# A separate account for row maxima beside a two-layer MLP, and a later division: a gated mix of sliding-window attention and MLP

## The chip, the cores and the metric

The kernel runs on one core of one Trainium2 chip. The metric is the device time of one execution in microseconds (us), lower is better. TensorE (PE, with its weight loads PEld), VectorE (DVE), ScalarE (ACT) and GpSimd (POOL) compute; SyncE (SP) issues the DMAs in the order of the program.

## The reference

The input is a sequence of 2048 rows of 512 values in fp32. Two branches are computed and mixed row by row with a gate.

```python
g = sigmoid((x * gate_w).sum(-1, keepdims=True))
# A: attention, 32 heads of 16, each query sees itself and the 255 keys before it
q, k, v = heads(x @ wqkv)                       # wqkv 512 x 1536
p = softmax(where(mask, q @ k.T * 16 ** -0.5, -1e9))
a = merge(p @ v) @ wo                           # wo 512 x 512
# B: MLP, hidden width 1792
h = gelu_tanh(x @ w1 + b1)
b = h @ w2 + b2
return g * a + (1 - g) * b
```

## The kernel before

**Staging.** The rows are cut in four tiles of 512. Large products run as three matmuls on a high and a low half of each operand (`mm3`, L108 to L110): first q, k and v of all tiles (`qkv`), then the MLP in eight turns of half the hidden width and one tile each (`mlp`), then the product with `wo` (`final`). A turn has two stages. In the first, u, seven blocks of x times w1 are made, and each goes through `gelu` (L715): four steps on ACT and three on DVE (L725, L731, L737). In the second, y, the seven results are multiplied with w2 into four output blocks, which DVE evicts (L812). `stage[0]` tells which of the two is being issued.

**Attention.** It is issued between these products, in 128 blocks: eight head groups of four heads, each over 16 blocks of 128 rows. A block has four steps, and for each step there are two things. `att_max` (L508) makes a score product `sm` (L519) on PE whose row maximum DVE takes (L524, into `M`); `att_exp` (L553) makes a score product `st` (L564) with the maximum already subtracted, whose exponential ACT takes (L586, into `pt`), and POOL masks it (L580; in the last blocks DVE does, L574). When four blocks of maxima are complete, `att_rows` (L530) turns them into rows of the second operand `qs`: three steps on DVE (L536 to L539), then eight copies on POOL (L546). `att_pvs` (L592) multiplies the exponentials of six blocks with v once in four blocks, into two accumulators, `pv_st` and `pv_sm`, which ACT and DVE evict into `nd` (L629, L632). `sm` and `st` have three PSUM buffers each, and a `pv` accumulator takes one of each kind.

**Division.** After two head groups `att_norm` (L642) divides: load the denominators (`den`, L646), reciprocal on DVE (L650, step `rcp`), store (L653, `keep`), load numerators and reciprocals (L658, `back`), multiply on DVE (L662, `mul`), store (L665). When each comes after the load of `den` stands in `DIVS` in nanoseconds, in one row for the last of the four passes and in one for the others. `load_part` (L695) loads the finished product `ot` (L703) and casts it into two halves on ACT (L706) and DVE (L709); for tile 0 the casts are planned `LAND0` after the load.

**Order.** The order on each engine is written out when the program is built. A planner keeps a clock, `now`, that each matmul advances by its planned length (`tick`); `after(ns, fn)` puts a step into a heap, and it is issued on its engine as soon as the clock passes its due time. The main loop goes through the steps of the blocks, and after each lets the dense products go on for a quarter of `STEP` (`fill`). In y and in the q, k, v stage it goes by pairs: both steps' scores, then both shares of dense work; in u each step stands alone. The block of maxima is always `LEAD` = 12 blocks ahead of the block of exponentials, so exactly one `sm` goes with one `st`. For the first 12 blocks there are maxima alone. The loads of `kd` and `qd`, the operands of `sm`, are issued by the block of maxima, those of `ks` and `vbuf` by the block of exponentials.

Of the kernel before, what the change touches and what calls it, by code (L numbers as in the profile page):

```python
# [19 lines left out]
NT = S // T  # L20
NB = T // 128
# [11 lines left out]
def gated_mix(ctx: ExitStack, tc: tile.TileContext, x, wqkv, wo, w1, b1, w2, b2, gate_w, out):  # L33
# [448 lines left out]
    def load_kd(g_, c):  # L482
        for t in range(max(c - 1, 0), c + 1):
            ready(t, g_, 1)
            k0 = 0 if t == c else T - W
            at = W if t == c else 0
            src = heads(SK[t], g_)[:, :, :, :, k0:].rearrange("s d u a c -> (s d u) a c")
            nc.sync.dma_start(f32(kd[0:96, slot(g_, c), :, at:at + T - k0]), src)

    def load_qd(g_, c):  # L490
        ready(c, g_, 0)
        put_pairs([f32(qd[48 * s:48 * s + 48, slot(g_, c)]) for s in range(2)], SQ[c], g_)

    def load_qs(g_, c):
        ready(c, g_, 0)
        need(("v", NT - 2, NB - 1))
        for s in range(2):
            v = f32(qs[64 * s + 4:64 * s + 52, :, c * T:(c + 1) * T])
            nc.sync.dma_start(v, part(SQ[c], g_, s).rearrange("r (a c) -> r a c", a=2))
# [8 lines left out]
    def att_max(g_, b, i):  # L508

        if b % RB == 0 and (g_, b // RB) not in Ms:  # L510
            Ms[g_, b // RB] = sb.tile([128, 2 * RB, 2], F32, tag="M", bufs=2, name=f"M{g_}_{b}")
        M = Ms[g_, b // RB]
        hb, pr = divmod(i, 2)
        c, n = b // NB, slot(g_, b // NB)
        j = 2 * (b % NB) + hb
        w = min(64 * (2 * b + hb + 1), W + 64)
        k1 = 64 * (j + 1) + W
        p = ps.tile([128, 320], F32, tag="sm", bufs=3, name=f"sm{g_}_{b}_{i}")
        nc.tensor.matmul(p[:, :w], qd[0:96, n, pr, 128 * j:128 * (j + 1)], kd[0:96, n, pr, k1 - w:k1],  # L519
                         start=True, stop=True)  # L520
        junk = cs.tile([128, 320], BF16, tag="jm", bufs=1, name=f"jm{g_}_{b}_{i}")

        def red():
            nc.vector.tensor_tensor_reduce(junk[:, :w], p[:, :w], mask[:, 320 - w:320], 1.0, -3e38,  # L524
                                           ALU.add, ALU.max, M[:, 2 * (b % RB) + hb, pr:pr + 1])
            done.add(("max", g_, b, i))
        tick(w / 2.4 + 13)
        after(100, red)
# [376 lines left out]
    stage = ["qk"]  # L905
# [3 lines left out]
    def fill(ns):  # L909

        owed[0] += ns
        while owed[0] > 0:
            c = next(run)
            if c is None:
                owed[0] = -1e9
            else:
                owed[0] -= c
                tick(c)

    NU = NG * NKB  # L920
    NQ = NG * NT
    fill(START - AHEAD)
    for c in (0, 1):
        load_qd(0, c)
    fill(AHEAD)
    for u in range(-LEAD, NU):
        m = u + LEAD
        gm, bm = divmod(m, NKB)
        step = STEP if u >= 0 else STEP0
        for i in range(4):  # L930
            if i == 1 and m % NB == 0 and NB <= m < NU - NB:
                load_kd(*divmod(m // NB + 1, NT)), load_qd(*divmod(m // NB + 1, NT))
            if i % 2 == 0:
                pair = (i, i + 1) if stage[0] != "u" else (i,)
            elif len(pair) == 2:
                continue
            else:
                pair = (i,)
            for op, i in [(op, k) for k in pair for op in ORDER[:3]] + [("f", k) for k in pair]:
                if op == "s" and u >= 0:  # L940
                    att_exp(u // NKB, u % NKB, i)
                if op == "m" and m < NU:
                    att_max(gm, bm, i ^ XOR)
                if op == "p" and i == PVAT and u >= 1:
                    att_pvs(u - 1)
                if op == "f":
                    fill(step / 4)
        if m < NU and bm % RB == RB - 1:
            after(900, att_rows, gm, bm // RB)
        if m % NB == QAT % NB and QAT <= m < QAT + NKB:  # L950
            load_qs(0, (m - QAT) // NB)
        if u % NB == 0 and NB <= u < NU - NB:
            load_ks(*divmod(u // NB + 1, NT))
        if u % NB == 2 and NB < u < NU - 3 * NB:
            load_qs(*divmod(u // NB + 3, NT))
        if u % NB == 0 and u >= 0:
# [14 lines left out]
RB = 4  # L971
NKB = S // 128
# [3 lines left out]
LEAD = 12  # L976
QAT = 5
# [2 lines left out]
YSWAP = 3  # L980
GELU = (700, 1500, 3600, 4600, 6000, 7000)
XAT = 3
ORDER = 'mspf'
XOR = 1
PACE = 4000.0
LAND = 7500.0
REACH = 2500.0
LAND0 = 13500.0
LANDO = 6500.0
HOLD = 4000.0  # L990
HOLDQ = 1500.0
HOLDO = 3000.0
DIVS = ((5000, 7500, 13500, 20000, 22000), (4500, 5700, 8500, 17000, 18500))
REST = 1000.0
MXAT = 5500.0
AHEAD = 9e3
# [1 line left out]
PVAT = 2  # L998
# [21 lines left out]
```

## Time and profile before

| | |
|---|---|
| median of 3 runs | 750.34 us (750.16 to 750.76) |
| the profiled execution | 748.76 us, its span 747.1 us |
| TensorE busy | 732.2 us, 98% of the span |
| VectorE busy | 521.9 us, 70% |
| ScalarE, GpSimd busy | 421.9 us (56%), 372.7 us (50%) |
| granted TensorE clock | full speed in every slice |

In the profile's rows a number after L is a line of the kernel before, `out<-in` are tiles, and what stands in square brackets is idle time of the engine ahead of the instruction and who ended it. PEld is the weight load ahead of a matmul; it runs beside the matmul before. A matmul's end in the trace is modelled, so the time from one start to the next says more than the duration.

### The profile page before, as it was taken

How to read it: one execution, taken by the hardware profiler on the slowest of the kernel's cores; microseconds unless marked ns; L12 is line 12 of the kernel's file. 1: busy time of each engine (PE TensorE's matmuls, PEld its weight loads, DVE VectorE, ACT ScalarE, POOL GpSimd, SP SyncE). 2: the span in 40 equal slices, each digit the busy share in tenths (PEclk: the TensorE clock that was granted, in tenths of full speed). 3: DMA queues.
4: the chain of work that ended last, by engine and by line, in shares of the span. 5: the costliest groups of instructions: out<-in, count | busy, mean ns of one | idle time of the engine just before them, and what ended most of it. 6: DMA issues, size and time to landing. Idle time of an engine off the chain costs nothing.

```text
span 747.1 us, 17982 instructions
## 1 busy us (share of the span) xinstructions
PE 732.2 (98%) x6129; PEld 605.4 (81%) x6129; DVE 521.9 (70%) x1567; ACT 421.9 (56%) x972; POOL 372.7 (50%) x846
## 2 busy tenths in 40 slices
PE   9999999998999999999999999999999999999998
PEld 7888888876788888888887887888888888878787
DVE  4532325799768867986798689767867886784562
ACT  4434532358537844864695478447735853785541
POOL 4200000339756865786577667747765875630000
PEclk9999999999999999999999999999999999999999
DMA  9889798998895688799576989996799788538673
GB/s 324 322 275 403 256 395 279 257 321 182 257 269 139 158 235 212 183 225 268 149 174 153 228 227 227 259 244 150 180 276 234 205 227 224 136 89 263 215 268 127
DMA packets 179259, 172.12 MB, mean 230 GB/s; under 512 B 56672, under 2 KB 122976, under 8 KB 179168
## 3 DMA queue, kind: packets, MB, share of 16 engines
q1 hardware_dynamic: 179168, 170.97, 80.8%
q8 instruction: 49, 0.80, 0.5%
q14 instruction: 42, 0.34, 0.1%
HBM read 108.53 MB, written 62.39 MB: 229 GB/s over the span
## 4 chain that ended last, share of the span: by engine, by line
PE 84%; DMA 6%; DVE 3%; ACT 3%; issue 2%; SPq 1%; POOL 1%; DVEq 0%; ACTq 0%; POOLq 0%
PE sm L519 9%; PE st L564 8%; PE pv_sm L608 7%; PE y L108 6%; PE y L109 6%; PE y L110 6%; PE u L108 6%; PE u L109 5%; PE u L110 5%; PE qk L110 4%; PE qk L108 4%; PE qk L109 4%; PE v L108 2%; PE a L110 2%; PE v L110 2%
## 5 line engine op out<-in xcount | busy, mean ns | idle before, releaser
L524 DVE CUSTOM_DVE_ANT_0 jm<-sm,mask 128x320 bf16<-128x320 f32 (+4 forms) x512 | 238.5, 466 | 95.3 <-PE sm L519 58.9
L586 ACT ACTIVATE pt<-st 128x320 f32<-128x320 f32 (+4 forms) x512 | 199.7, 424 | 140.2 <-PE st L564 137.8
L580 POOL TENSOR_SCALAR_AFFINE_SELECT pt<-pt 64x256 f32<-64x256 f32 (+1 forms) x538 | 225.3, 439 | 106.7 <-ACT pt L586 96.5
L519 PE MATMUL sm<-kd,qd 96*128 96x320 f32 (+4 forms) x512 | 153.4, 311 | 6.2 <-DVE M L524 4.7
L564 PE MATMUL st<-qs,ks 128*128 128x320 f32 (+4 forms) x512 | 154.2, 309 | 1.0 <-ACT pt L586 1.0
L546 POOL CAST qs<-tt 4x256 fp32r<-4x256 f32 x256 | 127.3, 497 | 53.0 <-DVE tt L539 42.4
L519 PEld LDWEIGHTS sm<-kd,qd 96*128 96x128 f32 x512 | 96.4, 188 | 31.3 <-DVE M L524 10.7
L564 PEld LDWEIGHTS st<-qs,ks 128*128 128x128 f32 x512 | 97.3, 190 | 18.1 <-ACT pt L586 2.3
L108 PE MATMUL y<-w,h 128*128 128x512 f32 x224 | 88.5, 395 | 0.0
L109 PE MATMUL y<-w,h 128*128 128x512 f32 x224 | 88.0, 393 | 0.0
L110 PE MATMUL y<-w,h 128*128 128x512 f32 x224 | 87.9, 392 | 0.0
L108 PE MATMUL u<-mx,w 128*128 128x512 f32 x196 | 79.9, 408 | 0.0
L109 PE MATMUL u<-mx,w 128*128 128x512 f32 x196 | 77.3, 395 | 0.0
L110 PE MATMUL u<-mx,w 128*128 128x512 f32 x196 | 77.1, 393 | 0.0
L608 PE MATMUL pv_st<-pt,vbuf 64*32 64x320 f32 (+4 forms) x1408 | 73.2, 346 | 1.0 <-ACT pt L586 1.0
L608 PE MATMUL pv_sm<-pt,vbuf 64*32 64x320 f32 (+4 forms) x1408 | 73.8, 346 | 0.1
L608 PEld LDWEIGHTS pv_sm<-pt,vbuf 64*32 64x32 f32 x1408 | 50.2, 106 | 19.9 <-issue 2.3
L325 DVE TENSOR_TENSOR qke<-qk,qke 128x512 fp32r<-128x512 f32 x32 | 22.1, 689 | 46.8 <-ACT qke L322 36.8
L322 ACT ACTIVATE qke<-qk 128x512 fp32r<-128x512 f32 x32 | 19.1, 598 | 55.5 <-PE qk L110 36.5
L110 PEld LDWEIGHTS y<-w,h 128*128 128x128 f32 x224 | 42.1, 188 | 9.7
L338 POOL MEMSET vx<- 128x32 f32 x16 | 2.4, 154 | 89.6 <-DMA SQ<-qke 43.7
L608 PEld LDWEIGHTS pv_st<-pt,vbuf 64*32 64x32 f32 x1408 | 45.7, 106 | 1.1 <-ACT pt L586 1.1
(148 smaller groups left out, 1335.5 us busy)
## 6 DMA issues: line engine op xcount, KB each, us to landing
kd<-SK SPq DMA_DIRECT2D x32, 384.0 KB
qs<-SQ SPq DMA_DIRECT2D x64, 192.0 KB
mx<-XT SPq DMA_DIRECT2D x24, 512.0 KB
SQ<-qke SPq DMA_DIRECT2D x16, 512.0 KB
SK<-qke SPq DMA_DIRECT2D x16, 512.0 KB
ND<-nd SPq DMA_DIRECT2D x32, 256.0 KB
raw_w<-in_B_w_dram SPq DMA_DIRECT2D x28, 256.0 KB
ks<-SK SPq DMA_DIRECT2D x32, 192.0 KB
```

Source lines behind the costliest of these rows:

```text
L108: nc.tensor.matmul(p, lh, rh, start=first, stop=False)
L109: nc.tensor.matmul(p, lh, rl, start=False, stop=False)
L110: nc.tensor.matmul(p, ll, rh, start=False, stop=last)
L322: nc.scalar.activation(e[:, h], p, AF.Copy)
L325: nc.vector.tensor_sub(e[:, 1 - h], p, f32(e[:, h]))
L519: nc.tensor.matmul(p[:, :w], qd[0:96, n, pr, 128 * j:128 * (j + 1)], kd[0:96, n, pr, k1 - w:k1], start=True, stop=True)
L524: nc.vector.tensor_tensor_reduce(junk[:, :w], p[:, :w], mask[:, 320 - w:320], 1.0, -3e38, ALU.add, ALU.max, M[:, 2 * (b % RB) + hb, pr:pr ...
L546: nc.gpsimd.tensor_copy(dst, src.unsqueeze(1).broadcast_to([4, 2, RB, 32]))
L564: nc.tensor.matmul(p[:, :w], ks[:, slot(g_, kb // NB), pr, at:at + 128], qs[:, pr, k0:k0 + w], start=True, stop=True)
L580: nc.gpsimd.affine_select(out=v, in_=v, pattern=[[0, v.shape[1]], [1 - 2 * e, 64]], compare_op=ALU.is_ge, fill=0.0, base=-e, channel_multi ...
L586: nc.scalar.activation(pt[:, hf, pr, :w], p[:, :w], AF.Exp, scale=SCALE)
L608: nc.tensor.matmul(pv[r // 64][32 * i:32 * i + 32, q - c * T:e - c * T], vts[g_, b // NB][r:r + 64, v:v + 32], rhs(r), start=start, stop=s ...
```

## The change

Maxima get an account of their own. `maxima(at)` is called at each step of the exponentials with the step's number. It credits the account with `MAXIMA` of the current stage (0.86 in u, 1.16 in y; 1 before the exponentials begin) and issues one maximum for each whole credit, and no more than two credits are kept. `LEADS` bounds how far maxima are ahead of exponentials: at least 10 and at most 12 blocks. The loads of `kd`, `qd` and of the first group's `qs`, and `att_rows`, are tied to the maxima's own count; `att_rows` is due 1400 ns after a batch's last maximum instead of 900 after the block. Apart from that, the first row of `DIVS` is later in all steps, by 3000 ns for the reciprocal, the product and its store and by 2500 for the two between, and `LAND0` is 2500 ns shorter.

```diff
+    made, credit = [0], [0.0]
+    def next_max():
+        m, i = divmod(made[0], 4)
+        made[0] += 1
+        gm, bm = divmod(m, NKB)
+        if i == 1 and m % NB == 0 and NB <= m < NU - NB:
+            load_kd(*divmod(m // NB + 1, NT)), load_qd(*divmod(m // NB + 1, NT))
+        att_max(gm, bm, i ^ XOR)
+        if i == 3 and bm % RB == RB - 1:
+            after(1400, att_rows, gm, bm // RB)
+        if i == 3 and m % NB == QAT % NB and QAT <= m < QAT + NKB:
+            after(600, load_qs, 0, (m - QAT) // NB)
+    def maxima(at):
+        credit[0] = min(credit[0] + (MAXIMA[stage[0]] if at >= 0 else 1), 2)
+        low, high = at + 4 * LEADS[0], min(at + 4 * LEADS[1] + 1, 4 * NU)
+        while made[0] < high and (credit[0] >= 1 or made[0] < low):
+            credit[0] -= 1
+            next_max()
     for u in range(-LEAD, NU):
...
-            for op, i in [(op, k) for k in pair for op in ORDER[:3]] + [("f", k) for k in pair]:
-                if op == "s" and u >= 0:
-                    att_exp(u // NKB, u % NKB, i)
-                if op == "m" and m < NU:
-                    att_max(gm, bm, i ^ XOR)
-                if op == "p" and i == PVAT and u >= 1:
+            for k in pair:
+                maxima(4 * u + k)
+                if u >= 0:
+                    att_exp(u // NKB, u % NKB, k)
+                if k == PVAT and u >= 1:
                     att_pvs(u - 1)
-                if op == "f":
-                    fill(step / 4)
-        if m < NU and bm % RB == RB - 1:
-            after(900, att_rows, gm, bm // RB)
-        if m % NB == QAT % NB and QAT <= m < QAT + NKB:
-            load_qs(0, (m - QAT) // NB)
+            for k in pair:
+                fill(step / 4)
...
-ORDER = 'mspf'
+MAXIMA = {"qk": 1.0, "u": 0.86, "y": 1.16, "a": 1.0}
+LEADS = (10, 12)
...
-LAND0 = 13500.0
+LAND0 = 11000.0
...
-DIVS = ((5000, 7500, 13500, 20000, 22000), (4500, 5700, 8500, 17000, 18500))
+DIVS = ((8000, 10000, 16000, 23000, 25000), (4500, 5700, 8500, 17000, 18500))
```

What this does to the order is shown at three places. The first is on PE in the first u stage, where the exponentials begin. `sm0_12_1` is the maximum's product of head group 0, block 12, step 1; `st0_0_0` is the exponential's of group 0, block 0, step 0; `u3_2` is a block of the MLP's first product. Before:

```order
L519 MATMUL sm0_12_1_1770<-kd_76,qd_75 128x320
L564 MATMUL st0_0_0_1774<-qs_73,ks_74 128x320
L108 MATMUL u3_2_1740<-xt3_1009,w1_2_1418 128x512
L109 MATMUL u3_2_1740<-xt3_1009,w1_2_1418 128x512
L110 MATMUL u3_2_1740<-xt3_1009,w1_2_1418 128x512
L519 MATMUL sm0_12_0_1789<-kd_76,qd_75 128x320
L564 MATMUL st0_0_1_1794<-qs_73,ks_74 128x320
```

After the change, on PE at the same place:

```order
L564 MATMUL st0_0_0_1770<-qs_73,ks_74 128x320
L108 MATMUL u3_2_1740<-xt3_1009,w1_2_1426 128x512
L109 MATMUL u3_2_1740<-xt3_1009,w1_2_1426 128x512
L110 MATMUL u3_2_1740<-xt3_1009,w1_2_1426 128x512
L519 MATMUL sm0_12_1_1781<-kd_76,qd_75 128x320
L564 MATMUL st0_0_1_1784<-qs_73,ks_74 128x320
```

The first `st` goes without an `sm`, and every later maximum comes a step later. Every seventh or eighth step of a u stage is like this, and about as many steps of a y stage have two `sm`.

The second place is on DVE late in the fifth turn's u stage, where head group 4's first `pv` group is evicted (`nd4_0`). `num2_1` and `den3_1` are of the division, `h2_10`, `x1h2_11` and `sqh2_11` of the GELU, `w2_12` of a weight split; `jm5_0_1` is the maximum of head group 5, block 0, step 1, and the row after it reads it out. Before:

```order
L725 SCALAR_TENSOR_TENSOR sqh2_11_6553_6560<-sqh2_11_6553_6560,x1h2_11_6553_6559 128x512
L662 TENSOR_TENSOR num2_1_6467<-num2_1_6467,rb2_1_6469 128x512
L650 RECIPROCAL den3_1_6498<-den3_1_6498 128x32
L737 TENSOR_TENSOR h2_10_6472<-x1h2_10_6472_6478,h2_10_6472 128x512
L182 TENSOR_TENSOR w2_12_6617<-raw_w212_6446,w2_12_6617 128x512
L632 TENSOR_TENSOR nd4_0_6620<-nd4_0_6620,pv4_0_sm_6573 128x512
L524 ISA jm5_0_2_6630,M5_0_6520<-sm5_0_2_6628,mask_72 128x128
```

After the change, on DVE:

```order
L737 TENSOR_TENSOR h2_10_6460<-x1h2_10_6460_6466,h2_10_6460 128x512
L182 TENSOR_TENSOR w2_12_6595<-raw_w212_6444,w2_12_6595 128x512
L632 TENSOR_TENSOR nd4_0_6597<-nd4_0_6597,pv4_0_sm_6552 128x512
L524 ISA jm5_0_1_6608,M5_0_6605<-sm5_0_1_6606,mask_72 128x64
L524 ISA M5_0_6605 128x1
L524 ISA jm5_0_0_6634,M5_0_6605<-sm5_0_0_6632,mask_72 128x64
L524 ISA M5_0_6605 128x1
L731 SCALAR_TENSOR_TENSOR x1h2_11_6532_6538<-sqh2_11_6532_6539,x1h2_11_6532_6538 128x512
L524 ISA jm5_0_3_6647,M5_0_6605<-sm5_0_3_6645,mask_72 128x128
L524 ISA M5_0_6605 128x1
L662 TENSOR_TENSOR num2_1_6501<-num2_1_6501,rb2_1_6503 128x512
L650 RECIPROCAL den3_1_6489<-den3_1_6489 128x32
```

The eviction now stands ahead of the division's two steps, and of three maxima that used to be ahead of it.

The third place is on DVE at the end of the last y stage. `ot0` is the loaded attention result of tile 0, `pt7_15` the last exponentials, `yo3_13` the MLP's last output block. Before:

```order
L574 TENSOR_TENSOR pt7_15_10452<-pt7_15_10452,cut_159 128x2x64
L662 TENSOR_TENSOR num1_3_10368<-num1_3_10368,rb1_3_10370 128x512
L574 TENSOR_TENSOR pt7_15_10452<-pt7_15_10452,cut_159 128x2x64
L812 SCALAR_TENSOR_TENSOR yo3_13_10488<-y3_13_10416,ya3_13_10366 128x512
L709 TENSOR_TENSOR ot0_10291<-ot0_10291 128x512
L650 RECIPROCAL den2_3_10437<-den2_3_10437 128x32
L709 TENSOR_TENSOR ot0_10291<-ot0_10291 128x512 x2
```

After the change, on DVE:

```order
L709 TENSOR_TENSOR ot0_10291<-ot0_10291 128x512
L574 TENSOR_TENSOR pt7_15_10453<-pt7_15_10453,cut_159 128x2x64
L709 TENSOR_TENSOR ot0_10291<-ot0_10291 128x512
L662 TENSOR_TENSOR num1_3_10368<-num1_3_10368,rb1_3_10370 128x512
L709 TENSOR_TENSOR ot0_10291<-ot0_10291 128x512
L574 TENSOR_TENSOR pt7_15_10453<-pt7_15_10453,cut_159 128x2x64
L812 SCALAR_TENSOR_TENSOR yo3_13_10493<-y3_13_10416,ya3_13_10366 128x512
L650 RECIPROCAL den2_3_10437<-den2_3_10437 128x32
```

The three casts of `ot0` have moved ahead of the reciprocal, and two of them ahead of the last masking that they used to follow.

More of the change, by code (lines that the diff above doesn't have):

```diff
@@ L925, in gated_mix @@
     fill(AHEAD)
+    made, credit = [0], [0.0]
[16 more added lines that the diff above has]
+            next_max()
     for u in range(-LEAD, NU):
-        m = u + LEAD
-        gm, bm = divmod(m, NKB)
         step = STEP if u >= 0 else STEP0
         for i in range(4):
-            if i == 1 and m % NB == 0 and NB <= m < NU - NB:
-                load_kd(*divmod(m // NB + 1, NT)), load_qd(*divmod(m // NB + 1, NT))
             if i % 2 == 0:
```

## The prediction

> **What bounds the kernel now.** I read the page first: the engines' busy shares and the shares of the chain that ended last.
>
> ```profile
> PE 732.2 (98%) x6129; PEld 605.4 (81%) x6129; DVE 521.9 (70%) x1567; ACT 421.9 (56%) x972; POOL 372.7 (50%) x846
> PE 84%; DMA 6%; DVE 3%; ACT 3%; issue 2%; SPq 1%; POOL 1%; DVEq 0%; ACTq 0%; POOLq 0%
> ```
>
> TensorE is busy for 732.2 of 747.1 us, and the change takes no matmul away, so only its waits can be won. The next view is the busy time by stage; the cuts are where the products u (the MLP's first) and y (its second) begin in the timeline. The columns are stretch, length, then busy us of PE, PEld, DVE, ACT, POOL, then the granted clock.
>
> ```profile
> core 0: us, PE busy (x) PEld busy (x) DVE busy (x) ACT busy (x) POOL busy (x), PEclk, DMA share, GB/s
> 151.20:185.50 34.30, 31.44 (x209) 24.31 (x208) 31.71 (x94) 25.07 (x52) 21.80 (x38) 1.00 0.92 240
> 185.50:221.00 35.50, 34.53 (x345) 28.72 (x344) 24.69 (x86) 17.05 (x42) 24.40 (x62) 1.00 0.92 266
> 289.10:322.20 33.10, 33.10 (x318) 27.84 (x317) 29.62 (x93) 25.56 (x58) 22.69 (x47) 1.00 0.76 187
> 356.90:391.20 34.30, 33.64 (x318) 27.90 (x317) 30.25 (x92) 27.17 (x62) 22.92 (x48) 1.00 0.67 161
> 391.20:426.90 35.70, 34.51 (x342) 28.46 (x341) 27.27 (x91) 18.28 (x44) 25.40 (x61) 1.00 0.76 183
> 426.90:462.80 35.90, 34.50 (x320) 28.09 (x319) 32.53 (x99) 28.02 (x64) 24.87 (x48) 1.00 0.93 226
> 497.50:531.50 34.00, 33.80 (x320) 28.23 (x319) 26.62 (x89) 25.51 (x57) 22.82 (x50) 1.00 0.61 150
> ```
>
> Every stage is alike in its work for TensorE. PE has no idle time in the u of 289 to 322, where DVE is busy for 29.62 of 33.10 us. It idles where DVE also splits weights: 2.86 + 0.97 us in the first u and y, 0.66 + 1.19 in 357 to 427, 1.40 in 427 to 463. The waits by who waited for whom say the same; the first row is of the whole run; those below it are of the stretches 160:190, 375:400, 430:470 (two rows) and 500:640, in that order, and the last is of 375:400.
>
> ```profile
> PEld sm L519 <- DVE M L524: 10.7, 20, 1.2
> ...
> PEld sm L519 <- DVE M L524: 6.4, 12, 1.2
> PEld sm L519 <- DVE M L524: 2.1, 3, 1.2
> PEld sm L519 <- DVE M L524: 1.6, 4, 0.6
> PEld sm L519 <- DVE nd L632: 1.7, 1, 1.7
> PEld sm L519 <- DVE M L524: 0.6, 1, 0.6
> ...
> PEld pv_st L608 <- ACT pt L586: 0.9, 1, 0.9
> ```
>
> A score product `sm` has three buffers, so it waits until DVE has taken the maximum (L524, result `M`) of the third one back. The 20 waits of its weight load, 10.7 us (the first row), all lie in these four stretches. How much of such a wait is lost shows one of them:
>
> ```profile
> 397.88 0.31 PE L564 MATMUL st<-qs,ks 128*128 128x320 f32 x1
> 399.11 0.42 PE L519 MATMUL sm<-kd,qd 96*128 96x320 f32 x1 [0.92 <-DVE M L524]
> 399.36 0.31 PE L564 MATMUL st<-qs,ks 128*128 128x320 f32 x1
> 399.51 0.39 PE L108 MATMUL y<-w,h 128*128 128x512 f32 x1
> ```
>
> The regular step from a 320-column product to the next is 0.15 us (399.36 to 399.51). Here it is 1.23, so 1.08 is lost, where PE's idle time says 0.92 and PEld's 1.2. I take nine tenths of PEld's: 5.8, 1.9, 3.0 (with 1.7 for `nd`) and 0.5 us, 11.2 in all. That is the ceiling of the main part.
>
> **The change, part by part.** *Fewer maxima in u.* By the order of the instructions the first u stage holds 28 `sm` instead of 31, the next six 28 or 29 instead of 32 or 33; the 27 taken out follow in the y stages (36 to 38 instead of 32 to 34). What one costs on DVE is read from the start of one to the start of what follows it:
>
> ```profile
> 158.02 0.49 DVE L524 CUSTOM_DVE_ANT_0 jm<-sm,mask 128x320 bf16<-128x320 f32 x1
> 158.67 0.49 DVE L524 CUSTOM_DVE_ANT_0 jm<-sm,mask 128x320 bf16<-128x320 f32 x1
> ...
> 395.84 0.48 DVE L524 CUSTOM_DVE_ANT_0 jm<-sm,mask 128x320 bf16<-128x320 f32 x1
> 396.25 0.68 DVE L737 TENSOR_TENSOR h<-x1h,h 128x512 fp32r<-128x512 f32 x1
> ```
>
> It costs 0.64 us ahead of another maximum and 0.41 ahead of another operation; both stand in these stages, so I take the middle, 0.53. Three fewer are 1.6 us (1.2 to 1.9), four fewer 2.1 (1.6 to 2.6). Where DVE is late all through, PE gets this one for one. That gives **-1.6** in the first u, under its ceiling of 5.8; **-1.9** in 357 to 400, where the ceiling is the smaller; **-0.4** at 500 to 531. In the stages without idle time it gives nothing. For PE itself the move costs nothing: 0.15 us leave u and come back in y.
>
> *The division.* Its steps for all passes but the last (first row of `DIVS`) come 2.5 to 3 us later. At 458 this takes a product and a reciprocal out of the way of `nd` (L632), which frees the buffer that `sm` waits for:
>
> ```profile
> 455.26 0.69 DVE L662 TENSOR_TENSOR num<-num,rb 128x512 f32<-128x512 f32 x1
> 455.87 0.34 DVE L650 RECIPROCAL den<-den 128x32 f32<-128x32 f32 x1
> 456.13 0.62 DVE L737 TENSOR_TENSOR h<-x1h,h 128x512 fp32r<-128x512 f32 x1
> 456.68 0.87 DVE L182 TENSOR_TENSOR w<-raw_w,w 128x512 fp32r<-128x512 f32 x1
> 457.48 0.67 DVE L632 TENSOR_TENSOR nd<-nd,pv_sm 128x512 f32<-128x512 f32 x1
> ```
>
> From 455.26 to 456.13 that is 0.87 us; with the 2.1 of the maxima it fills the ceiling of 3.0. I take **-2.5**, since part of the relief falls after the last wait. Between reciprocal and `keep` (L653) SP now has 2.0 instead of 2.5 us: 12 issues may each hold SP's queue 0.5 us longer, with the loads behind them. I cost that at nothing, because no row has PE waiting for a load; if that cover went, it would be up to 6 us of SP time, not of PE's.
>
> *What moves along.* `att_rows` (three DVE steps, eight POOL copies) comes after one or two maxima more, and its consumer `st` never waits for POOL in the rows of PE; the lead is still 11 blocks at its lowest, a batch of rows is needed by 5 to 6 blocks, and a block takes some 4 us (33.10 us hold 32 `st`, four to a block), so five blocks cover it and it costs nothing; uncovered it would be the three DVE steps, under 1 us each time. The loads of `kd` and `qd` (four or five DMAs a tile) follow the maxima, up to four steps later, together with their users, 16 maxima ahead of them as before; `load_qs` of the first head group (two DMAs) is issued 0.6 us later. On SP they pass the loads of `ks` and `vbuf` and some of the division's issues. SP stands at the `kd` load for long anyway:
>
> ```profile
> SPq L488 <- PE st L564: 53.3, 23, 7.0
> ```
>
> PE's waits name no DMA, so that queue has slack, and I cost it at nothing too; if it had none, a load later by two or three steps of some 1 us would show as that wait in PE.
>
> *The end.* `LAND0` puts three casts of `ot0` (L706, L709) 2.5 us earlier.
>
> ```profile
> 696.08 0.29 DVE L574 TENSOR_TENSOR pt<-pt,cut 128x128 f32<-128x128 f32 x1
> ...
> 699.97 0.35 DVE L650 RECIPROCAL den<-den 128x32 f32<-128x32 f32 x1 [2.08 <-DMA den<-ND]
> ...
> 699.62 0.40 PE L108 MATMUL a<-wo,ot 128*128 128x512 f32 x1
> 699.85 0.39 PE L109 MATMUL a<-wo,ot 128*128 128x512 f32 x1
> 700.93 0.50 PE L110 MATMUL a<-wo,ot 128*128 128x512 f32 x1 [0.69 <-DVE ot L709]
> ```
>
> Before, two of the casts stood behind a reciprocal that waited for its load until 699.97; a product began 1.08 us after the one before it (699.85 to 700.93), where 0.23 is regular (699.62 to 699.85). That 0.85 goes. In exchange the last masking of the exponentials (L574, 696.08), for which the last `pv` group is due, comes behind casts, each about as long as the L662 above (0.61 from 455.26 to 455.87): 0.6 if one more comes between, 1.2 if two push it, nothing if DVE's queue leaves that much room. I take one, 0.6: **-0.3**, rounded up.
>
> *What it adds.* In y, 27 steps have two `sm` in a row. One stands right behind a `pv` group, where L632 then comes one maximum later. If none waits it is 0; if all wait, 27 x 0.53 = 14.3. It is nearer to 0, for in y DVE has 10 us free of 35.5 (24.69 busy), and DVE waits for PE more often than PE for it:
>
> ```profile
> DVE jm L524 <- PE sm L519: 41.1, 66, 2.3
> ```
>
> I take two that wait: **+1.0**. ACT gets no relief, and u is shorter: in 427 to 463 its share goes from 28.02 of 35.9 us (78%) to 28.02 of about 33 (85%): **+0.3**.
>
> Sum: -1.6 - 1.9 - 2.5 - 0.4 - 0.3 + 1.0 + 0.3 = -5.4 us. The profiled execution took 748.76 us (span 747.1 and 1.7 around it): 743.4. Against the median of 750.34, 1.6 above it, the forecast is **744.9**. A difference of 0.2%, 1.5 us, is about what can be told from none.
>
> *A rule against it.* DVE and POOL get in each other's way, as rows at 160 show:
>
> ```profile
> 159.94 1.62 POOL L182 TENSOR_TENSOR w<-raw_w,w 128x512 fp32r<-128x512 f32 x1 [6.77 <-ACT w L178]
> 160.42 1.70 DVE L725 SCALAR_TENSOR_TENSOR sqh<-sqh,x1h 128x512 f32<-128x512 f32 x1
> ...
> L725 DVE SCALAR_TENSOR_TENSOR sqh<-sqh,x1h 128x512 f32<-128x512 f32 x41 | 31.7, 772 | 2.2 <-ACT sqh L722 1.7
> ```
>
> L725 takes 0.77 us on average and took 1.70 when a POOL product ran from 159.94 to 161.56. The Trainium skill (SBUF — State Buffer, Who interferes with whom) says that a DVE instruction with two SBUF inputs contends with a GpSimd instruction that reads SBUF, and one with a single SBUF input does not; the row at 160.42 agrees. By that rule the maxima, which read one operand from PSUM, are what DVE can do freely beside POOL, and taking them out of u leaves the GELU's operations denser against POOL's; by it the sum would lose the terms of u and come out near no change.
>
> **The rivals.** *The relief is lost to POOL (no change).* A u stage has 21 GELU operations on DVE. At 0.77 us each they take 16.2; if the denser queue put each beside POOL, at the 0.87 of the L182 row above, they would take 18.3. These 2.1 us are just what four maxima free. Left would be the division's 0.9 and the end's 0.3 against the 1.3 added: 750.4. For it: POOL is busy for two thirds of a u stage (22.92 of 34.30). Against it: at that share the 0.77 already holds the collisions there are, and POOL's work stays the same.
>
> *The doublings make y wait (slower).* The mechanism is the third `sm` buffer: of two `sm` in a row the second, or the next pair's, finds DVE one maximum late. Each that waits costs 0.53 us; the gains of 6.4 are used up at 12 of 27. With two in three, 18 x 0.53 = 9.5, it is 6.4 less, so +3.1: 753.4. For it: the first 5 to 10 us of y are where the waits at 399.11 and after 463 stand, and DVE enters y late. Against it: y's free third on DVE, and that it enters y 1.6 to 2.1 us less late.
>
> *The counts don't come out* (the change does nothing): excluded by the order, 27 moved.
>
> **How the numbers follow.** The forecast has 0.74. Its own range goes from all terms at their best, with most of the 0.9 us that `pv_st` waits for `pt` beside the second (-1.9 - 2.6 - 3.0 - 0.5 - 0.9 = -8.9: 741.4) to half the relief and four waits in y (-3.2 + 2.1 = -1.1: 749.2), of which the last 0.03 counts as no change. A deeper gain, if the first u loses more waits than its three maxima pay for, has 0.04; no change 0.10; slower 0.12. The range reaches from the best terms to the no-change case, 741.4 to 750.4, and leaves out 0.16. Faster by over 0.2% is 0.74 - 0.03 + 0.04 = 0.75, the same 0.10 + 0.03 = 0.13, slower 0.12.
>
> **What would show it.** Right: in the busy time by stage of the changed kernel PE's idle time in 357 to 463 shrinks from 3.2 to under 1 us and in the first u from 2.9 to about 2; the weight loads of `sm` waiting for `M` fall from 10.7 to about 5 us; L632 at about 455 runs ahead of L662; no wait of `a` for `ot` at 700, and a short one of the last `pv` for L574. Wrong: new waits of `sm` in y behind doubled rows, GELU operations that take 0.85 us and more on average, or a wait of PE on a load.

## The result, and the profile after

The changed kernel takes 754.91 us (median of 6 runs, 754.41 to 755.89) against 750.55 us of the kernel before on the same chip: a ratio of 1.0052, with an interval of 1.0036 to 1.0069. It is slower by about 4 us, where the forecast was 744.9. The profiled execution took 754.41 us, its span 752.6, 5.5 more than before; about 1 us of that is scatter, since the profiled execution before, 748.76 us, was faster than its median. First two lines of the page after: the busy shares, and the shares of the chain that ended last.

```profile
PE 733.9 (98%) x6129; PEld 607.9 (81%) x6129; DVE 523.2 (70%) x1567; ACT 422.3 (56%) x972; POOL 367.6 (49%) x846
...
PE 78%; DVE 5%; DMA 5%; ACT 4%; POOL 3%; issue 3%; SPq 2%; DVEq 0%; ACTq 0%; POOLq 0%
```

No engine has noticeably more to do. TensorE's share of the chain fell from 84% to 78%, and DVE, ACT and POOL have 5, 4 and 3% where they had 3, 3 and 1: more often TensorE waits for one of them. The busy time by stage, columns as in the prediction:

```profile
151.50:186.20 34.70, 31.15 (x207) 24.46 (x206) 30.99 (x88) 24.87 (x52) 19.40 (x34) 1.00 0.90 242
186.20:221.80 35.60, 34.72 (x346) 29.00 (x346) 24.68 (x90) 17.15 (x42) 25.35 (x65) 1.00 0.97 254
...
359.30:393.80 34.50, 33.03 (x314) 27.14 (x313) 29.40 (x86) 26.81 (x62) 21.86 (x46) 1.00 0.63 157
393.80:429.90 36.10, 34.98 (x346) 28.88 (x345) 28.43 (x97) 18.34 (x44) 25.81 (x63) 1.00 0.72 187
429.90:464.50 34.60, 33.57 (x315) 27.38 (x314) 31.16 (x89) 27.52 (x63) 23.15 (x44) 1.00 0.94 226
...
501.20:534.10 32.90, 32.90 (x316) 27.64 (x316) 25.68 (x81) 25.45 (x57) 21.28 (x46) 1.00 0.58 144
534.10:572.00 37.90, 35.98 (x348) 29.62 (x347) 26.98 (x95) 16.67 (x41) 24.75 (x63) 1.00 0.85 212
```

The u stages lost DVE work as foreseen (32.53 to 31.16 us in the fifth, 26.62 to 25.68 in the sixth), and some are shorter by about the matmuls that left them. The first is not: 34.70 us against 34.30, with 3.55 idle against 2.86. The y stages are longer, most of all the sixth turn's, 37.90 us. That stage of the kernel before took:

```profile
531.50:565.60 34.10, 34.10 (x345) 28.54 (x343) 25.10 (x87) 16.35 (x41) 23.41 (x58) 1.00 0.97 253
```

Who waited for whom; the first two rows are of the kernel before, the others of the changed one:

```profile
PEld pv_sm L608 <- POOL pt L580: 0.5, 2, 0.2
PEld pv_sm L608 <- DVE M L524: 0.2, 1, 0.2
...
PEld sm L519 <- DVE M L524: 8.5, 14, 1.4
...
PEld st L564 <- ACT pt L586: 3.5, 8, 1.3
...
PEld pv_sm L608 <- DVE M L524: 3.1, 10, 0.7
...
PEld pv_sm L608 <- POOL pt L580: 2.1, 5, 0.6
```

The waits of `sm` for maxima fell from 10.7 to 8.5 us only. The news is in the waits of `pv`: for POOL's masks (L580) and for DVE's maxima (`M`), because a `pv` accumulator takes over buffers of `sm` that DVE has to empty first. The page's two groups of `pv` matmuls show them as well; first before, then after. The last two numbers are PE's idle time ahead of them, and of it what the named releaser ended.

```profile
L608 PE MATMUL pv_st<-pt,vbuf 64*32 64x320 f32 (+4 forms) x1408 | 73.2, 346 | 1.0 <-ACT pt L586 1.0
...
L608 PE MATMUL pv_sm<-pt,vbuf 64*32 64x320 f32 (+4 forms) x1408 | 73.8, 346 | 0.1
```

```profile
L608 PE MATMUL pv_sm<-pt,vbuf 64*32 64x320 f32 (+4 forms) x1408 | 75.6, 347 | 1.6 <-POOL pt L580 0.9
...
L608 PE MATMUL pv_st<-pt,vbuf 64*32 64x320 f32 (+4 forms) x1408 | 74.5, 347 | 2.4 <-POOL pt L580 1.2
```

Such idle numbers hide part of it, because a group's matmuls run overlapped (in the last fence of this section 0.25 to 0.30 us each, several at a time). I measured each of the 32 groups from the start of the instruction ahead of it to the start of the one behind it. Groups are named by head group and tile; the columns e6, e8 and e11 are runs told below.

| us | before | after | e6 | e8 | e11 |
|---|---|---|---|---|---|
| `pv0_0` | 2.20 | 4.81 | 2.20 | 3.02 | 2.20 |
| `pv1_1` | 2.57 | 3.09 | 2.57 | 3.23 | 2.57 |
| `pv2_1` | 2.56 | 2.94 | 2.97 | 3.60 | 2.59 |
| `pv5_1` | 2.57 | 4.00 | 4.02 | 6.50 | 2.57 |
| `pv7_3` | 2.65 | 3.43 | 3.46 | 2.91 | 3.42 |
| all 32 | 82.3 | 88.2 | 84.4 | 97.0 | 83.0 |

The growth is 5.9 us, and it has four parts. 2.6 us are `pv0_0`, whose masks are late for a reason of its own (told at the end, under the first u). 2.0 us are `pv1_1` and `pv5_1`, whose weight loads wait for POOL's masks. 1.2 us are `pv2_1`, `pv6_1` (3.39 for 2.93) and `pv1_2` (2.88 for 2.56), which wait for `M`. 0.8 us are `pv7_3`, which the earlier casts of `LAND0` delay. The other groups are 0.6 us shorter in sum. Around the groups, steps that began over 0.13 us later than the median distance of such a pair of lines (after 150 us) cost `sm` 7.7 us instead of 8.5, `st` 3.2 instead of 1.8, `a` nothing instead of 0.8: the sum is 5.9 - 0.8 + 1.4 - 0.8 = 5.7, for 5.5 us of span.

Where `pv5_1` waits is read from POOL's timeline, first before, then after:

```profile
520.73 3.49 POOL L546 CAST qs<-tt 4x256 fp32r<-4x256 f32 x6
525.46 2.18 POOL L580 TENSOR_SCALAR_AFFINE_SELECT pt<-pt 64x256 f32<-64x256 f32 x4 [1.23 <-ACT pt L586]
527.71 0.83 POOL L546 CAST qs<-tt 4x256 fp32r<-4x256 f32 x2
528.60 2.30 POOL L580 TENSOR_SCALAR_AFFINE_SELECT pt<-pt 64x256 f32<-64x256 f32 x4
531.90 5.44 POOL L580 TENSOR_SCALAR_AFFINE_SELECT pt<-pt 64x256 f32<-64x256 f32 x12 [1.00 <-ACT pt L586]
```

```profile
526.06 0.82 POOL L546 CAST qs<-tt 4x256 fp32r<-4x256 f32 x2 [1.77 <-DVE tt L539]
528.68 1.84 POOL L580 TENSOR_SCALAR_AFFINE_SELECT pt<-pt 64x256 f32<-64x256 f32 x4 [1.79 <-ACT pt L586]
530.58 3.12 POOL L546 CAST qs<-tt 4x256 fp32r<-4x256 f32 x5
533.77 2.39 POOL L580 TENSOR_SCALAR_AFFINE_SELECT pt<-pt 64x256 f32<-64x256 f32 x4
536.22 0.93 POOL L546 CAST qs<-tt 4x256 fp32r<-4x256 f32 x1
537.22 4.67 POOL L580 TENSOR_SCALAR_AFFINE_SELECT pt<-pt 64x256 f32<-64x256 f32 x12
```

Before, six of the eight copies of the maxima (L546) ran ahead of the first block's masks, in a time when POOL then still waited for ACT, and the masks ended at 537.34, 0.2 us before the `pv` group began at 537.52. After, the maxima are up to one block less ahead (11 to 12 blocks, by the order of the products), so the copies come later against the masks: six of them stand behind the first block's masks and ahead of the second's and third's. The masks then end at 541.89, and PE, which began the group at 540.25, waits inside it:

```profile
540.25 0.30 PE L608 MATMUL pv_sm<-pt,vbuf 64*32 64x64 f32 x2
541.11 0.30 PE L608 MATMUL pv_st<-pt,vbuf 64*32 64x64 f32 x4 [0.57 <-POOL pt L580]
541.70 0.25 PE L608 MATMUL pv_sm<-pt,vbuf 64*32 64x64 f32 x2 [0.28 <-POOL pt L580]
```

### The profile page after: what moved, and what is told of

It reads as the page before. It is cut to its first block, busy times and chain, and to the rows that moved or that the text cites. A ratio compares the mean times of both kernels' runs of the same rounds, so it can differ in the third digit from the quotient of the medians.

```text
span 752.6 us, 17944 instructions
## 1 busy us (share of the span) xinstructions
PE 733.9 (98%) x6129; PEld 607.9 (81%) x6129; DVE 523.2 (70%) x1567; ACT 422.3 (56%) x972; POOL 367.6 (49%) x846
## 4 chain that ended last, share of the span: by engine, by line
PE 78%; DVE 5%; DMA 5%; ACT 4%; POOL 3%; issue 3%; SPq 2%; DVEq 0%; ACTq 0%; POOLq 0%
PE sm L519 8%; PE st L564 7%; PE pv_sm L608 7%; PE u L108 6%; PE u L109 5%; PE u L110 5%; PE y L109 5%; PE y L108 5%; PE y L110 5%; PE qk L110 4%; PE qk L108 4%; PE qk L109 4%; POOL pt L580 2%; PE a L108 2%; PE v L108 2%
## 5 line engine op out<-in xcount | busy, mean ns | idle before, releaser
L580 POOL TENSOR_SCALAR_AFFINE_SELECT pt<-pt 64x256 f32<-64x256 f32 (+1 forms) x538 | 225.7, 439 | 102.6 <-ACT pt L586 91.4
L519 PE MATMUL sm<-kd,qd 96*128 96x320 f32 (+4 forms) x512 | 148.7, 310 | 5.6 <-DVE M L524 4.1
L546 POOL CAST qs<-tt 4x256 fp32r<-4x256 f32 x256 | 121.4, 474 | 66.8 <-DVE tt L539 55.9
L109 PE MATMUL y<-w,h 128*128 128x512 f32 x224 | 88.2, 394 | 0.0
L608 PE MATMUL pv_sm<-pt,vbuf 64*32 64x320 f32 (+4 forms) x1408 | 75.6, 347 | 1.6 <-POOL pt L580 0.9
L608 PEld LDWEIGHTS pv_sm<-pt,vbuf 64*32 64x32 f32 x1408 | 52.5, 106 | 20.8 <-DVE M L524 2.6
L608 PEld LDWEIGHTS pv_st<-pt,vbuf 64*32 64x32 f32 x1408 | 47.4, 106 | 3.1 <-POOL pt L580 1.6
L725 DVE SCALAR_TENSOR_TENSOR sqh<-sqh,x1h 128x512 f32<-128x512 f32 x56 | 43.1, 769 | 4.6 <-ACT sqh L722 4.2
```

The costliest lines, as they stand in the source:

```text
L109: nc.tensor.matmul(p, lh, rl, start=False, stop=False)
L546: nc.gpsimd.tensor_copy(dst, src.unsqueeze(1).broadcast_to([4, 2, RB, 32]))
L580: nc.gpsimd.affine_select(out=v, in_=v, pattern=[[0, v.shape[1]], [1 - 2 * e, 64]], compare_op=ALU.is_ge, fill=0.0, base=-e, channel_multi ...
L608: nc.tensor.matmul(pv[r // 64][32 * i:32 * i + 32, q - c * T:e - c * T], vts[g_, b // NB][r:r + 64, v:v + 32], rhs(r), start=start, stop=s ...
L725: nc.vector.scalar_tensor_tensor(sq, sq, GC, x1, op0=ALU.add, op1=ALU.mult)
```

## The experiments

They ran in four sets, each beside the kernel before on the same chip, whose medians were 750.58 to 751.64 us; a ratio is to that median. Three theories: **copies** (in the expectations "POOL", "masks", and with VectorE's row steps "order"): `att_rows` moved, and with it what `pv` waits for. **Doublings** ("bunches"): two `sm` in a row cost more than was taken out of u. **Division**: its steps or `LAND0` do it.

**Which part of the change does it?** e1 is the changed kernel without the last two parts, e2 and e3 are the kernel before with one of them each, e4 is the changed kernel with even steps.

```diff
 e1_account: changed, with
-LAND0 = 11000.0
+LAND0 = 13500.0
-DIVS = ((8000, 10000, 16000, 23000, 25000), ...
+DIVS = ((5000, 7500, 13500, 20000, 22000), ...
 e2_division: before, with DIVS as changed
 e3_land0: before, with LAND0 as changed
 e4_even: changed, with
+MAXIMA = {"qk": 1.0, "u": 1.0, "y": 1.0, "a": 1.0}
```

> The account alone (division and LAND0 as before). Theory POOL: the uneven maxima put the copies of the rows among the masks of the blocks that pv needs, so the pv groups together stay about 5 us longer than before (88 instead of 82 us) and the time is 753 to 755. Theory doublings: the waits are those of sm in y; pv groups near 82 us, sm waits of 10 us and more, time again 753 to 755. Theory division: the loss comes from the division, so this kernel is at 746 to 749.

> The later division alone. Theory POOL: it moves neither copies nor masks; within 1 us of before, 749.5 to 751.5. Theory division: 753 or more, with DVE waiting for the loads of the product (L662) or of the reciprocal as in the changed kernel at 564.

> LAND0 alone. By the prediction's step: the wait of a for ot (0.85) goes, the last pv group waits 0.6 to 0.8 longer for its mask: 749.9 to 750.6 against 750.4. If the casts hurt more than they help: 751 or more.

> The changed kernel with a credit of 1.0 in every stage: one sm to each st as before, but rows due 1400 ns after their last maximum, later division, LAND0 short. Theory POOL: what matters is that uneven maxima shift the rows' copies against the masks; pv groups at 82 to 84 us, time 748 to 751. If the 1400 ns alone moves the copies into the way, pv groups near 88 and 753 to 755. Theory doublings: no doubles, so before's time less the division's gain, 749 to 750.

Measured: e1 755.45 us (ratio 1.0068, 1.0044 to 1.0093), e2 751.41 (1.0011, 0.9994 to 1.0029), e3 750.33 (0.9994, 0.9981 to 1.0008), e4 751.97 (1.001, 0.9996 to 1.0024). So the uneven account makes the loss, and neither of the others by itself does anything that can be measured. e1 and the changed kernel hardly differ, so the division's later times bring nothing with this account either. The `pv` groups of e1 are long in the same places as in the changed kernel (86.9 us in all, `pv0_0` 4.81, `pv5_1` 4.00). In e4 they take 84.9 us, a little over the 84 expected: its copies stand as early as before or earlier, but its `pv` groups wait 3.5 us for `M`. So not all of the groups' growth is the copies'.

**Do the copies cost that much?** e8 is the kernel before with nothing but `att_rows` one block later. On POOL one to three copies then stand ahead of the second block's masks in nearly every group of four blocks, and the others behind them. That is more than the change does: in the changed kernel one group is like this (`pv1_1`'s), in 11 of some 30 one or two copies stand ahead of the *first* block's masks and the others behind them, and in the rest four or more stand ahead. Of these twelve groups only `pv1_1` and `pv5_1` then wait longer for masks. The three row steps on DVE move along too.

```diff
-        if m < NU and bm % RB == RB - 1:
-            after(900, att_rows, gm, bm // RB)
+        r = u + LEAD - 1
+        if 0 <= r < NU and r % RB == RB - 1:
+            after(900, att_rows, r // NKB, r % NKB // RB)
```

> The kernel before, with nothing of the change, but att_rows called one block later: then GpSimd's eight copies stand between the masks of the first three blocks of each group of four (two or three copies, the masks of the second block, five or six copies, the masks of the third), the order in which they stand in about a third of the groups of the changed kernel. Theory 'masks': the masks of a group's last block end 1 to 2.5 us later, the pv groups grow by 4 us or more in sum, and the time rises to 753.5 to 758. Theory 'bunches': the copies' place costs nothing, as the prediction had it: 750.2 to 751.0.

Measured: 769.21 us, ratio 1.024 (1.0209 to 1.0271), 18.6 us slower, far more than the 3 to 7.5 us that the theory said. The page of e8:

```profile
PE 67%; POOL 12%; DMA 6%; ACT 5%; DVE 5%; issue 3%; SPq 1%; DVEq 0%; ACTq 0%; POOLq 0%
...
L608 PE MATMUL pv_sm<-pt,vbuf 64*32 64x320 f32 (+4 forms) x1408 | 79.1, 352 | 6.1 <-POOL pt L580 5.7
```

POOL's part of the chain goes from 1 to 12%, the groups of `pv` from 82.3 to 97.0 us. An edit that moves three row steps and eight small copies by one block, the copies on an engine that is busy half of the time, costs four times what the whole change costs. It shows that the place of the copies can cost this much, not what it costs in the changed kernel.

**Is the loss gone when the copies are put back?** e5 is the changed kernel with the copies at their old place between the masks, for maxima four blocks older, since the account does not promise newer ones there. e6 is the changed kernel with even steps until block 16, e7 is both.

```diff
 e5_rows_fixed
-        if i == 3 and bm % RB == RB - 1:
-            after(1400, att_rows, gm, bm // RB)
+        r = u + 8
+        if 0 <= r < NU and r % RB == RB - 1:
+            att_rows(r // NKB, r % NKB // RB)      # its copies 900 later than PUT says
 e6_second
-        credit[0] = min(credit[0] + (MAXIMA[stage[0]] if at >= 0 else 1), 2)
+        credit[0] = min(credit[0] + (MAXIMA[stage[0]] if at >= 4 * FROM else 1), 2)
...
+FROM = 16
```

> The changed kernel, with att_rows called again at a fixed place, the end of every fourth block, for the group of maxima four blocks older, so that GpSimd's eight copies stand where they stand in the kernel before: behind the last masks of one group of four blocks and ahead of, or just behind, the first masks of the next. The account, DIVS and LAND0 stay as changed. Theory 'masks' (the account loses because the copies now stand between masks that a pv group waits for): the pv groups, 88.2 us in the changed kernel and 82.3 before, come back except for the first one (+2.6, whose masks wait for something else) and the last (+0.8): 85.5 to 86.0 us, and the time falls from 754.9 to about 752.5 (751.8 to 753.2). Theory 'bunches' (the doubled maxima and their moved work cost it on TensorE and VectorE, wherever the copies stand): pv groups may shrink, but the time stays at 754.2 to 755.5.

> The changed kernel, with every step of the account worth 1.0 until the attention's fifth group of four blocks (block 16); from there u counts 0.86 and y 1.16 as changed. The copies of the maxima are not put back. Theory 'masks': the first pv group goes back from 4.8 to 2.2 us, because GpSimd's split of w2_3 stands again ahead of the second block's masks, but the waits for maxima in the first u stage come back too (3.1 us lost against 0.6), so that the time hardly moves: 754.0 to 755.2, with the y stage of the sixth turn as long as in the changed kernel (37.9). Theory 'first stage' (the relief of the first u stage is real and the loss lies elsewhere): 756 to 757.

> Both edits together: copies at their fixed place, and the account even until block 16. Theory 'masks': pv groups at 83 to 84 us, the time at 751.0 to 752.5. Theory 'bunches': 754 to 755.5, since the doubled maxima of seven of the eight turns are still there.

Measured: e5 758.34 us (1.0097, 1.0068 to 1.0125), e6 752.84 (1.0025, 1.0008 to 1.0041), e7 757.26 (1.0082, 1.0055 to 1.0108). In e5 the `pv` groups came down to 83.9 us, further than expected, and the time rose all the same, which neither theory had; e7, with 83.9 us too, missed both in the same way. A row of PE in e5 tells why:

```profile
173.61 0.42 PE L564 MATMUL st<-qs,ks 128*128 128x320 f32 x1 [3.40 <-POOL qs L546]
```

Four blocks later the copies are too late for `st`: its weight loads wait 7.5 us for L546 in all (6.3 in e7), and here PE loses 3.4 at once. So the copies have to come in time for `st` and yet not among the masks; of the places tried only the old one does both. e6 gave the first group back (2.20 us) and was 2 us faster than the changed kernel, not the same as I had expected: the relief in the first u stage had been worth less than what it cost.

**With every order kept, do uneven maxima gain?** e9 sets `LEADS` to 12.25 and 14 (by the order of its products the maxima are 12 to 13 blocks ahead), so that the copies can stand in their old place for the newest maxima; e10 is the same with even steps.

```diff
 e9_ahead
-LEADS = (10, 12)
+LEADS = (12.25, 14)
-        if i == 3 and bm % RB == RB - 1:
-            after(1400, att_rows, gm, bm // RB)
+        r = u + LEAD
+        if 0 <= r < NU and r % RB == RB - 1:
+            att_rows(r // NKB, r % NKB // RB)      # its copies 900 later than PUT says
 e10_ahead_even: e9 with MAXIMA 1.0 in u and y
```

> The changed kernel with the maxima led by 12.25 to 14 blocks instead of 10 to 12, and att_rows called at the end of every fourth block for the group just made: GpSimd's copies then stand as in the kernel before (behind the last masks of a group of four blocks, six to eight copies ahead of or around the first masks of the next), and they come as early before their st as there, so that st does not wait for them as it did at the place four blocks later. The account's 0.86 and 1.16 hold from the second u stage on (in the first the lead cannot fall below its lower bound). Theory 'masks' (all of the account's loss is the copies' place): pv groups at 82.5 to 84.5 us and the time at 749.5 to 751.3. Theory 'bunches' (doubled maxima in the y stages make TensorE wait there too): pv groups as said, but waits of sm in y stay at 3 us or more beyond those of the kernel before, and the time at 752 to 753.5.

> The same, with every step of the account worth 1.0: the maxima in even steps, 12.25 blocks ahead, DIVS and LAND0 as changed. Both theories: 750.2 to 751.5, pv groups at 82.5 to 84. What the run before this one differs from it is what uneven steps bring by themselves: theory 'masks' 0.5 to 1.5 us less with uneven steps, theory 'bunches' 1 to 3 us more.

Measured: e9 753.68 us (1.0027, 1.0009 to 1.0046), e10 754.72 (1.0039, 1.0021 to 1.0058). The `pv` groups take 86.5 and 87.6 us, more than either theory said, and uneven steps are 1.0 us faster than even ones, within the intervals. Both theories missed e10 by 3 us: its maxima are as even as before, its copies stand as before, and it was slow. What was left was VectorE: here `att_rows` issued its three steps at once instead of 900 ns later on the planner's clock. e14 is the kernel before with that alone; e11 is e9 with `after(900, att_rows, ...)`, so that GpSimd's order is that of the kernel before in every instruction; e12 is e11 with `DIVS` and `LAND0` as before.

```diff
 e14_steps_early: before, with
-            after(900, att_rows, gm, bm // RB)
+            att_rows(gm, bm // RB)                 # its copies 900 later than PUT says
 e11_order_kept: e9, with
-            att_rows(r // NKB, r % NKB // RB)      # its copies at PUT again
+            after(900, att_rows, r // NKB, r % NKB // RB)
```

> The kernel before with att_rows called at once instead of 900 later on the planner's clock, the copies held at their old times: TensorE, GpSimd and the DMA queues keep their orders, and VectorE's three row steps stand right behind the last reduction of their group, some two reductions earlier. It asks what made the run e10_ahead_even slow, whose maxima are as even as before and whose copies stand as before. Theory 'order' (the row steps ahead of a reduction that a pv group's bank waits for): 752.5 to 753.5. Otherwise 750.3 to 751.2.

> The changed kernel with the maxima led by 12.25 to 14 blocks and att_rows called, 900 later on the planner's clock, at the end of every fourth block, exactly as in the kernel before: GpSimd's instructions then stand in the same order as in the kernel before, all of them, and VectorE's three row steps stand where they stood too. Uneven account from the second u stage on, DIVS and LAND0 as changed. Theory 'order' (all of the loss comes from where the copies on GpSimd and the row steps on VectorE went; the uneven maxima by themselves gain): 749.3 to 751.0. Theory 'bunches' (uneven maxima lose by themselves): 752 to 754.

> The kernel before with the uneven account alone, led by 12.25 to 14 blocks, the copies and row steps in their old places, DIVS and LAND0 as before: GpSimd's order is that of the kernel before, instruction for instruction, and what differs is the place of the maxima on TensorE and of their reductions on VectorE. Theory 'order': 749.0 to 750.6, pv groups at 82 to 83.5. Theory 'bunches': 751.5 to 753.5.

Measured: e14 755.37 us (1.0062, 1.0038 to 1.0087). TensorE, GpSimd and the DMA queues have the order of the kernel before; three short steps stand a few places earlier on VectorE, and 4.7 us are lost, more than the 1.9 to 2.9 that the theory said (in its trace the `pv` groups take 86.8 us, 4.5 more than before). The same stretch on VectorE before, then in e14, then TensorE in e14 and all such waits of e14:

```profile
451.83 0.22 DVE L524 CUSTOM_DVE_ANT_0 jm<-sm,mask 128x64 bf16<-128x64 f32 x1
...
452.58 0.26 DVE L536 TENSOR_SCALAR nm<-M 128x16 fp32r<-128x16 f32 x1
```

```profile
456.35 0.27 DVE L536 TENSOR_SCALAR nm<-M 128x16 fp32r<-128x16 f32 x1
456.65 0.21 DVE L537 SCALAR_TENSOR_TENSOR nm<-M,nm 128x16 fp32r<-128x16 f32 x1
456.96 0.45 DVE L539 STREAM_TRANSPOSE tt<-nm 128x256 f32<-128x256 f32 x1
457.33 0.18 DVE L524 CUSTOM_DVE_ANT_0 jm<-sm,mask 128x64 bf16<-128x64 f32 x1
```

```profile
457.58 0.24 PE L608 MATMUL pv_sm<-nil,vbuf 64*32 64x64 f32 x1 [0.60 <-DVE M L524]
...
PEld pv_sm L608 <- DVE M L524: 7.3, 19, 1.0
```

The three steps take 0.98 us (456.35 to 457.33). In the kernel before the reduction of 64 columns stood ahead of them (451.83); here it stands behind (457.33), and `pv_sm`, which needs the buffer that it empties, waits for it. The changed kernel has less of the same: by the order on VectorE its row steps stand right behind their batch's last reduction in 17 of 32 batches, where one is like this before and all are in e14. Its `pv_sm` weight loads wait 3.1 us for `M`, those of the kernel before 0.2, those of e14 7.3 (much of it hidden beside other work).

e11 took 751.40 us, ratio 1.0007 (0.9993 to 1.002): no difference from the kernel before, and its `pv` groups are back at 83.0 us. With the order around the `pv` groups kept and the division later, the account, uneven from the second u stage on, loses nothing and gains nothing. The fourth turn of e11:

```profile
357.50:390.70 33.20, 33.01 (x315) 27.59 (x314) 29.08 (x87) 27.13 (x62) 23.87 (x47) 1.00 0.71 170
390.70:427.70 37.00, 35.22 (x346) 28.90 (x345) 28.57 (x97) 18.46 (x44) 25.03 (x61) 1.00 0.75 181
```

Its u is 1.1 us shorter than before (33.20 for 34.30), its y 1.3 longer (37.00 for 35.70). Of this, PE's idle time makes 0.47 less in u (0.19 for 0.66) and 0.59 more in y (1.78 for 1.19); most of the rest is the time of the products that moved. In all turns from the second to the seventh the two together stay within 0.3 us of before, but for the fifth with +1.1.

e12 took 757.45 us (1.0086, 1.0058 to 1.0115; its runs spread from 753.5 to 759.4, and the profiled one is the fastest, so its trace shows less than half of the loss). Both theories missed it: GpSimd's order is that of the kernel before, the `pv` groups take 82.1 us, and it is slow. So the account at this lead needs the division's later times, some 6 us between e11 and e12, where they were worth nothing at the old orders (e2) or in the changed kernel (e1); `LAND0` went back with them, which by e3 is nothing. In e12 the division's reciprocal on VectorE, then the `sm` behind it on TensorE, then the sum of such waits of VectorE (us, times, longest):

```profile
560.48 0.35 DVE L650 RECIPROCAL den<-den 128x32 f32<-128x32 f32 x1 [3.68 <-DMA den<-ND]
```

```profile
561.24 0.41 PE L519 MATMUL sm<-kd,qd 96*128 96x320 f32 x1 [1.52 <-DVE M L524]
```

```profile
DVE den L650 <- DMA den<-ND: 9.0, 4, 3.7
```

The reciprocal holds VectorE's queue for 3.68 us until its load lands, and the maxima behind it make TensorE wait. In e11, with the step 3 us later, the same sum is 4.4 us and this wait is gone. Why the load lands later is seen on SP's queue, first before, then in e12:

```profile
548.62 0.59 SPq L646 DMA_DIRECT2D den<-ND  x1
```

```profile
549.29 2.72 SPq L488 DMA_DIRECT2D kd<-SK  x2
...
554.72 0.60 SPq L646 DMA_DIRECT2D den<-ND  x1
```

The loads of `kd` and `qd` go with the maxima, which lead by more here, and now stand ahead of the load of `den`: it is issued 6.1 us later. No run changes this order alone. No version ran measurably faster than the kernel before.

## Why the prediction was wrong, point by point

Forecast and profile are 10.9 us apart (-5.4 against +5.5). 5.3 of them are the `pv` groups (5.9 us longer where 0.6 was forecast), 4.6 the relief of `sm` (0.8 us where 6.4 less 1.0 for doublings was forecast) and 1.1 the waits of `st` (1.4 for 0.3). So two steps failed. The smaller is that what moves along costs nothing: it cost 2.3 us in the `pv` groups. The larger is that PE gets the maxima's time in u one for one: the 4.6 did not come, and 2.6 of the `pv` groups' growth is the first u's relief taken back.

- **What moves along, "costs nothing": a step that failed.** It asked whether the copies come late for `st`. One row of the changed kernel names them (a weight load at 171.62, 1.2 us), but the matmul's own row there names ACT, and in the kernel before it starts at the same time (171.67). It did not ask what stands *behind* the copies on POOL's queue: the masks, and behind the masks `pv5_1` with 0.2 us of slack. Nor what stands behind the three row steps on DVE: it bounded them by "under 1 us each time", which is what one wait of e14 shows, but with all 32 batches moved they cost 4.7 us. The five blocks of cover were true for the data and irrelevant for the queue. The `pv` groups grew by 5.9 us; forecast was 0.6, for the last one's mask (0.8 measured). Of the rest, 2.0 are behind copies and masks on POOL (`pv1_1`, `pv5_1`) and 0.3 behind the row steps on DVE (`pv1_2`, where the steps run from 282.72 to 283.57 and the reduction comes next). The 0.8 of `pv2_1` and `pv6_1` are behind later maxima without row steps ahead of them, and the 2.6 of `pv0_0` belong to the next point. With the orders put back and the first u even (e11) the growth is 0.7 us, which is the last group's.
- **First u, -1.6: relieved and given back.** Time lost by `sm` there fell from 3.1 to 0.6 us, more than forecast. But `st` then waited for ACT's exponentials (1.06 to 2.23 us lost), and the first `pv` group, reached at 179.57 instead of 181.60, found the masks not done: on POOL the weight split (L182) now stands behind the second block's masks and ran at 176.26 instead of 173.29, and the masks ended at 183.99 instead of 183.21. The prediction took DVE's time for PE's ("PE gets this one for one") and did not ask what is late next once `sm` is on time. The run e6, with even steps in the first turn, is 2 us faster than the changed kernel. POOL there, before and after:

```profile
173.29 1.29 POOL L182 TENSOR_TENSOR w<-raw_w,w 128x512 fp32r<-128x512 f32 x1
174.53 8.68 POOL L580 TENSOR_SCALAR_AFFINE_SELECT pt<-pt 64x256 f32<-64x256 f32 x16
```

```profile
173.25 2.93 POOL L580 TENSOR_SCALAR_AFFINE_SELECT pt<-pt 64x256 f32<-64x256 f32 x4
176.26 1.81 POOL L182 TENSOR_TENSOR w<-raw_w,w 128x512 fp32r<-128x512 f32 x1
178.03 5.96 POOL L580 TENSOR_SCALAR_AFFINE_SELECT pt<-pt 64x256 f32<-64x256 f32 x12
```

- **357 to 400, -1.9, and 427 to 467, -2.5: mis-sized.** PE's idle time in 359 to 430 is 1.47 + 1.12 us against 0.66 + 1.19 before, in 430 to 464 1.03 against 1.40. The waits for `nd` (L632) went from 1.7 us to 2.0, though L632 does stand ahead of the division now. e11 shows why: PE's idle time that left u in the fourth turn (0.47 us) came back in y (0.59). For all of `sm` the time lost fell by 0.8 us (8.5 to 7.7), where the three points on u and the one at 500 (-0.4) had 6.4, and 5.4 with the doublings.
- **The end, -0.3.** Its parts were right: the wait of `a` is gone (0.8 us), and the last `pv` group waits for L574, 0.78 us longer. The two cancel: e3 750.33 us.

```profile
703.13 0.24 PE L608 MATMUL pv_st<-pt,vbuf 64*32 64x64 f32 x2 [0.48 <-DVE pt L574]
```

- **Doublings, +1.0, and the rival "make y wait".** About the right size, and not what made it slower by what the runs show: the rival forecast the sign for another reason. In y the second `sm` of a pair did wait once (468.80, 1.10 us). Three more waits, at 565 to 568 (1.55 us), came behind a step of the division that waited 1.85 us for its load. e11 has 21 doublings of the 27 and is level. What six more would cost at its orders was not tried.
- **ACT, +0.3: too small.** `st`, mostly behind ACT's exponentials, lost 1.4 us more.
- **The rival of POOL's contention** is refuted: of the GELU's steps on DVE, L725 took 769 ns on average in both kernels and L731 744; L737 took 768 for 757, 0.6 us over all 56. Where POOL cost time it did so by its order.

## What to carry to other kernels

When a step moves in a program with one in-order queue per engine, cost each queue it moves in by what then stands *behind* it and how much slack that has: late data for its own consumer is only half of the question. An idle half of an engine's time is no cover; ahead of `pv5_1` the cover was 0.2 us. And a relief is worth something only if the resource is free later: in e11 the waits that left u were back in y.

## What the runs showed that I had not expected

Eight copies of about 0.5 us and their three row steps, moved by one block, cost 18.6 us (e8), and the three row steps alone, together 0.98 us, moved by a few places cost 4.7 (e14), with no work added in either. And two parts that looked independent were not: the division's later times changed nothing by themselves (0.9994 to 1.0029) and nothing in the changed kernel (754.91 and e1's 755.45), but with the maxima led further the runs with and without them differ by 6 us (751.40 and 757.45).
